# Attention and two MoE layers in one kernel: three engines ordered by hand in chunks 1 to 5, preparations in three steps, PV's quarters laid out anew

## The chip, the cores and the metric

The kernel runs on one core of a Trainium2 chip. The metric is the device time of one launch in microseconds; the kernel before took 836.0 us, the median of 3 runs (834.54 to 841.95).

In the text PE is TensorE, DVE VectorE, ACT ScalarE, POOL GpSimd, and SP SyncE, whose queue issues nearly all the transfers.

## What is computed

```python
def reference(q, k, v, x_params):                    # 4 batches, 8 heads, 576 positions, head size 64
    s = q @ k.T / 8 + alibi; s[outside 0 <= i - j < 128] = -1e9
    x = softmax(s) @ v                               # heads side by side: 2304 tokens x 512
    x = ((x @ w_a) * (x @ w_b)) @ w_out              # 512 -> 1536 -> 512
    logits = x @ w_gate + modality_bias[modality_id] # 8 experts
    e = argmax(logits); p = softmax(logits)[e]
    return p * (relu(x @ w1[e]) @ w2[e])             # 512 -> 1024 -> 512, each token its own expert
```

All of it is float32.

## The kernel before

The 2304 tokens are 18 tiles of 128, in seven chunks of 3, 2, 2, 3, 3, 3 and 2 tiles (0 to 6). In a chunk the first MoE layer runs in 12 **slots** j, one for each 128 of its 1536 hidden features. A slot multiplies the chunk's tokens with a piece of w_a into the PSUM bank ab0 (`mm_ab`, 12 matmuls of 256 or 384 columns, since every factor is split into a rounded part and a rest, and three of the four products are taken), then with w_b into ab1 (12 more). ACT copies ab0 (`asb`, L1050), DVE multiplies ab1 with it (`gf`, L1054), ACT and DVE split the product into two parts (`g`, L1057 and L1058), and one slot later `mm_out` (L512) multiplies these with a piece of w_out into the accumulators acc0 to acc2. There is one buffer each of ab0, ab1, asb and gf, so the next A (the matmuls into ab0) waits until asb has read ab0, and the next B until gf has read ab1. Chunk 0 works with unsplit products (L508), which chunk 0's own weights preparation slows.

The attention of chunk c + 1 runs inside the slots of chunk c. Its unit is an **item**: one pair of heads and one tile of 128 tokens, 72 in all. For an item PE computes scores (4 matmuls, L244), DVE masks them and takes the minimum (L252, L258), ACT takes the exponentials (L268), DVE the inverse sums (L272, L273), ACT divides (L281), PE transposes (2, L294), ACT and DVE split the result (`pc`, L305 and L306), POOL masks it into `pt` (two selects, L308 and L310), PE multiplies with v (PV, 4 matmuls, L374), ACT copies the result to `u` (L378, one copy of 128 x 512), two transfers take two quarters of u to the other 64 partitions (`z`), and POOL adds: two adds of 64 x 128 (L386), then z (L388). The sum `xf` has one buffer for a whole chunk; `x_split` (L397, L398) makes from it the two parts of the next chunk's tokens.

Each pair of heads first needs its **preparations**: ACT and DVE split k (`kk`, L190 and L191), q in two halves of 64 partitions (`qq`, L213 and L214) and v (`vv`, L225 and L226). `a_preps` makes all of them in a row.

When a chunk is done, `evac_out` copies its accumulators to `x2` (L593, three buffers). In chunks 0 to 5 DVE then takes the router's logits as dot products with rows of w_gate laid out over the partitions (`rd_dot`, L579: 8 for each tile; `wgt` comes two experts at a time, 512 KB, in the ring of buffers tagged "wo"). `route_fin` ranks each tile's tokens by expert with two small matmuls (L555, L556) and writes x2 to DRAM (`x2d`, L546). Only then is that x2 buffer free again.

The order on the engines comes from a scheduler of the framework, which goes by priorities and its own estimate of the times. SP issues transfers in the order of its queue, each after what it waits for. After chunk 6 the 8 experts follow, one after the other.

Of the kernel before, what the change touches and what calls it, by code (L numbers as in the profile page):

```python
# [21 lines left out]
def attn_moe_moe2(ctx: ExitStack, tc, q, k, v, moe_w_a, moe_w_b, moe_w_out, modality_id,  # L22
# [162 lines left out]
    def a_prep_k(a):  # L185
        if a.c in S32:
            return
# [3 lines left out]
        (nc.gpsimd if KLP else nc.vector).tensor_tensor(out=a.kk[:, :, 1, :n], in0=a.kr[:, :, :n], in1=a.kk[:, :, 0, :n], op=ALU.subtract)  # L191

    def a_prep_q(a):
        n = a.nt * P
        if a.c in S32:
            if a.c > 0:
                a.qq = at.tile([P, 2, MT * P], F32, tag="qq", bufs=2, name="qq")
            for h in range(2):
                o, d = 64 * h, 64 * (1 - h)
                if a.c > 0:  # L200
                    nc.gpsimd.memset(a.qq[d:d + 64, h, :n], 0.0)
                if a.c == 0 and a.hp < QD and h == 1:
                    nc.vector.tensor_scalar(out=a.qq[o:o + 64, h, :n], in0=a.qr[o:o + 64, :n],
                                            scalar1=qscale[o:o + 64, a.hp:a.hp + 1], scalar2=None, op0=ALU.mult)
                    continue
                nc.scalar.activation(out=a.qq[o:o + 64, h, :n], in_=a.qr[o:o + 64, :n], func=AF.Copy,
                                     scale=qscale[o:o + 64, a.hp:a.hp + 1])
# [8 lines left out]

    def a_prep_v(a):
        nk = a.nt + 1
# [3 lines left out]
        a.vv = at.tile([P, MT + 1, 2, 2, D], F32R, tag="vv", bufs=2, name="vv")  # L222

        w = a.vv.rearrange("p t h r d -> p t (h r) d")
        nc.scalar.copy(out=w[:, :nk, 0::3, :], in_=a.vr[:, :nk])  # L225
        nc.vector.tensor_tensor(out=w[:, :nk, 1:3, :], in0=a.vr[:, :nk], in1=w[:, :nk, 0::3, :], op=ALU.subtract)  # L226
# [1132 lines left out]
```

## Time and profile before

| | |
|---|---|
| median of 3 runs (range) | 836.0 us (834.54 to 841.95) |
| the profiled execution | 837.88 us |
| its span, first to last instruction | 836.1 us |
| mean granted clock of TensorE | 0.987 of full speed |
| PE busy | 805.8 us, 96% of the span |
| DVE, ACT, POOL busy | 564.9, 428.8, 273.6 us |
| A of slot 0 of chunks 1 to 6 starts at | 143.5, 208.6, 278.3, 373.2, 468.4, 548.6 us |

The rows are read so: a matmul's time runs from its issue to its modelled end, and the next one starts before that, so the pace of PE is the distance between starts, not the mean time of one. Of a wait the profile names the last thing that ended it.

### The profile page before, as it was taken

How to read it: one execution, taken by the hardware profiler on the slowest of the kernel's cores; microseconds unless marked ns; L12 is line 12 of the kernel's file. 1: busy time of each engine (PE TensorE's matmuls, PEld its weight loads, DVE VectorE, ACT ScalarE, POOL GpSimd, SP SyncE). 2: the span in 40 equal slices, each digit the busy share in tenths (PEclk: the TensorE clock that was granted, in tenths of full speed). 3: DMA queues.
4: the chain of work that ended last, by engine and by line, in shares of the span. 5: the costliest groups of instructions: out<-in, count | busy, mean ns of one | idle time of the engine just before them, and what ended most of it. 6: DMA issues, size and time to landing. Idle time of an engine off the chain costs nothing.

```text
span 836.1 us, 14442 instructions
## 1 busy us (share of the span) xinstructions
PE 805.8 (96%) x4666; PEld 723.4 (87%) x4666; DVE 564.9 (68%) x1699; ACT 428.8 (51%) x1092; POOL 273.6 (33%) x401
## 2 busy tenths in 40 slices
PE   8999999999989999999999999999999999999994
PEld 6788787898889989998999999999988998989893
...
GB/s 246 339 408 187 149 123 179 194 278 222 160 240 188 176 209 190 134 114 143 168 168 116 88 158 144 189 161 234 120 83 301 198 192 133 168 137 313 102 27 40
DMA packets 76196, 148.79 MB, mean 178 GB/s; under 512 B 13711, under 2 KB 40495, under 8 KB 76112
## 3 DMA queue, kind: packets, MB, share of 16 engines
...
q8 instruction: 39, 0.64, 0.3%
q14 instruction: 45, 0.37, 0.2%
HBM read 122.35 MB, written 22.12 MB: 173 GB/s over the span
## 4 chain that ended last, share of the span: by engine, by line
PE 72%; issue 8%; DMA 7%; ACT 4%; DVE 4%; POOL 2%; SPq 1%; POOLq 0%; ACTq 0%; DVEq 0%
PE ps_ab L495 32%; PE acc L512 13%; PE ps_h L1112 7%; PE ps_y L1095 6%; PE acc L508 3%; PE ps_o L374 3%; PE ps_s L244 2%; DMA wgt<-in_wgt 2%; DMA wr<-in_moe_w 1%; PE ps_p L294 1%; PE ps_o L331 1%; DMA wraw<-in_moe_w_b 1%; PE ps_s L240 1%; DMA wos<-wo_f 1%; POOL out L1102 1%
## 5 line engine op out<-in xcount | busy, mean ns | idle before, releaser
L495 PE MATMUL ps_ab<-xr,wab 128*128 128x384 f32 (+1 forms) x2016 | 347.3, 319 | 7.8 <-DVE gf L1054 3.6
L495 PEld LDWEIGHTS ps_ab<-xr,wab 128*128 128x128 f32 x2016 | 310.7, 189 | 21.3 <-DVE gf L1054 4.8
L512 PE MATMUL acc<-wo,g 128*128 128x512 f32 x540 | 145.7, 399 | 0.6 <-ACT g L1057 0.6
L512 PEld LDWEIGHTS acc<-wo,g 128*128 128x128 f32 x540 | 96.7, 189 | 16.2 <-ACT g L1057 0.8
L308 POOL TENSOR_SCALAR_AFFINE_SELECT pt<-pc 128x512 fp32r<-128x512 f32 (+1 forms) x72 | 51.4, 713 | 172.1 <-ACT pc L300 68.0
L1112 PE MATMUL ps_h<-xT,w1s 128*128 128x384 f32 x576 | 104.3, 337 | 0.0
L1095 PE MATMUL ps_y<-w2s,h 128*128 128x512 f32 x432 | 104.0, 394 | 0.0
L579 DVE CUSTOM_DVE_ANT_0 junk<-x,wgt 128x512 f32<-128x512 f32 x128 | 94.0, 735 | 12.4 <-DMA wgt<-in_wgt 10.1
L1112 PEld LDWEIGHTS ps_h<-xT,w1s 128*128 128x128 f32 x576 | 99.7, 188 | 1.4 <-issue 0.5
L1095 PEld LDWEIGHTS ps_y<-w2s,h 128*128 128x128 f32 x432 | 79.7, 188 | 15.8
L386 POOL TENSOR_TENSOR xf<-u 64x128 f32<-64x128 f32 x104 | 65.6, 631 | 38.3 <-ACT u L378 16.5
L268 ACT ACTIVATE p<-p,mx 128x128 f32<-128x128 f32 x144 | 56.9, 397 | 28.9 <-DVE mx L258 28.2
L1057 ACT CAST g<-gf 128x256 fp32r<-128x256 f32 (+1 forms) x72 | 33.0, 458 | 61.8 <-DVE gf L1054 61.7
...
L1054 DVE TENSOR_TENSOR gf<-ps_ab,asb 128x256 f32<-128x256 f32 (+1 forms) x72 | 35.0, 486 | 30.6 <-PE ps_ab L495 28.2
L868 DVE TENSOR_TENSOR w2s<-wr,w2s 128x1024 fp32r<-128x1024 f32 x24 | 29.4, 1224 | 38.1 <-ACT w2s L867 37.8
...
L1050 ACT COPY asb<-ps_ab 128x256 f32<-128x256 f32 (+1 forms) x72 | 30.5, 424 | 46.2 <-PE ps_ab L495 45.9
L310 POOL TENSOR_SCALAR_AFFINE_SELECT pt<-pc 128x512 fp32r<-128x512 f32 (+1 forms) x72 | 53.2, 739 | 0.0
L868 DVE TENSOR_TENSOR w1s<-wr,w1s 128x1024 fp32r<-128x1024 f32 x28 | 34.3, 1224 | 24.1 <-ACT w1s L867 24.1
L1058 DVE TENSOR_TENSOR g<-gf,g 128x256 fp32r<-128x256 f32 (+1 forms) x72 | 39.8, 553 | 10.0 <-ACT g L1057 9.7
L281 ACT ACTIVATE p<-p,mx 128x128 f32<-128x128 f32 x104 | 36.0, 397 | 20.5 <-DVE mx L273 20.1
...
## 6 DMA issues: line engine op xcount, KB each, us to landing
wo<-wo_d SPq DMA_DIRECT2D x60, 512.0 KB, 4.1
wr<-in_moe_w SPq DMA_DIRECT2D x56, 512.0 KB, 4.3
wgt<-in_wgt SPq DMA_DIRECT2D x24, 512.0 KB, 4.4
wraw<-in_moe_w_a SPq DMA_DIRECT2D x12, 512.0 KB, 7.6
wraw<-in_moe_w_b SPq DMA_DIRECT2D x12, 512.0 KB, 8.0
wor<-in_moe_w_out SPq DMA_DIRECT2D x12, 512.0 KB, 4.8
...
wo_d<-wo SPq DMA_DIRECT2D x12, 512.0 KB, 3.7
```

The lines of the kernel that those rows point to most:

```text
L268: nc.scalar.activation(out=it.p[:, h, :], in_=it.p[:, h, :], func=AF.Exp, bias=it.mx[:, 2 + h:3 + h], scale=-1.0, accum_out=it.mx[:, 4 + h ...
L281: nc.scalar.activation(out=it.p[:, h, :], in_=it.p[:, h, :], func=AF.Copy, scale=it.mx[:, 6 + h:7 + h])
L308: nc.gpsimd.affine_select(out=it.pt[:, :, 0], in_=pc, pattern=pat + [[-1, P]], base=0, channel_multiplier=1, compare_op=ALU.is_gt, fill=0.0)
L310: nc.gpsimd.affine_select(out=it.pt[:, :, 1], in_=pc, pattern=pat + [[1, P]], base=0, channel_multiplier=-1, compare_op=ALU.is_ge, fill=0.0)
L386: nc.gpsimd.tensor_tensor(out=xf_t[a.c][o:o + 64, a.hp, n], in0=u[o:o + 64, h, 0:P], in1=u[o:o + 64, h, P:2 * P], op=ALU.add)
L495: nc.tensor.matmul(ps[:, :n], lhsT=w[:, m, r, kk * P:(kk + 1) * P], rhs=xr[:, s, kk, :n], start=(idx == 0), stop=(idx == len(terms) - 1))
L512: nc.tensor.matmul(acc[c, t], lhsT=g[:, r, t * P:(t + 1) * P], rhs=w[:, s, :], start=(j == 0 and idx == 0), stop=(j == NJ - 1 and idx == 2))
L579: nc.vector.tensor_tensor_reduce(out=junk, in0=x2[:, 0:DM], in1=wgt[:, k], scale=1.0, scalar=0.0, op0=ALU.mult, op1=ALU.add, accum_out=lgr ...
L868: nc.vector.tensor_tensor(out=dst[:, 1], in0=srcw, in1=dst[:, 0], op=ALU.subtract)
L1058: nc.vector.tensor_tensor(out=gt[:, 1, :n], in0=gf[:, :n], in1=gt[:, 0, :n], op=ALU.subtract)
L1095: nc.tensor.matmul(pss[t], lhsT=h[:, r, f, t * P:(t + 1) * P], rhs=W2[f // 2][:, s_, f % 2, :], start=(f == 0 and i == 0), stop=(f == 7 an ...
L1112: nc.tensor.matmul(ps, lhsT=W1[f // 2][:, r, kk, (f % 2) * P:(f % 2 + 1) * P], rhs=xT[:, s_, kk, :], start=(kk == 0 and i == 0), stop=(kk ...
```

## The change

In chunks 1 to 5 the order on PE, DVE and ACT is no longer the scheduler's. `step` writes a slot down, and `tc.manual_schedule` keeps the three engines to the written order (chunks 0 and 6 and the experts stay with the scheduler, POOL and SP too). A slot is: A, PV of the items of two slots ago, B, transposes of the last slot's items, scores of new ones, mm_out, one piece of a router. The list `goal` says how many items each slot starts: 50 in chunks 1 to 5, about one a slot, and only in the first nine slots of chunk 5.

- **Preparations in three steps.** k's first half (ACT) in one slot, q's in the next, v's shortly before it is needed; the DVE half of each follows a slot later (`new_preps`, `late_rests`).
- **PV's quarters.** PV writes so that u needs three quarters of 64 partitions for each head: two ACT copies of 64 x 384 in place of one of 128 x 512. Both heads then lie in their own partitions, and POOL does one add of 128 x 128 in place of two of 64 x 128. The add of z goes behind the next item's selects (`z_add`).
- **Routers.** The 5 tiles of chunks 0 and 1 are routed on PE (`route(..., late=True)`: 4 transposes and 4 matmuls each) in place of 40 dot products. Chunks 2 to 5 keep the dots, an expert a slot in slots 1 to 8; wgt has buffers of its own, one expert (256 KB) each, fetched two ahead.
- **x2d later.** The write of x2 (`gate`) comes after the ranks, one tile a slot in slots 9 to 11, where it used to come at about slot 3 or 4.
- **Buffers.** xf is one tile for a pair of heads (5 buffers); w_out's splitting works in place.
- The loads of the first expert's w1 begin in chunk 6; before, the scheduler had put part of them into chunk 5.

```diff
-    RD = (0, 1, 2, 3, 4, 5)
+    RD = (2, 3, 4, 5)
...
     def a_pv(it):
...
-        u = at.tile([P, 2, 2 * P], F32, tag="u", bufs=2, name="u")
-        nc.scalar.copy(out=u, in_=ps)
+        u = at.tile([P, 3, P], F32, tag="u", bufs=2, name="u")
...
         for h in range(2):
-            o, d = 64 * h, 64 - 64 * h
-            nc.sync.dma_start(out=z[o:o + 64], in_=u[d:d + 64, h, 0:P])
-        for h in range(2):
             o = 64 * h
-            nc.gpsimd.tensor_tensor(out=xf_t[a.c][o:o + 64, a.hp, n], in0=u[o:o + 64, h, 0:P],
-                                    in1=u[o:o + 64, h, P:2 * P], op=ALU.add)
-        nc.gpsimd.tensor_tensor(out=xf_t[a.c][:, a.hp, n], in0=xf_t[a.c][:, a.hp, n], in1=z, op=ALU.add)
+            nc.scalar.copy(out=u[o:o + 64], in_=ps[o:o + 64, 1 - h:4 - h])
+        for h in range(2):
+            o, d = 64 * h, 64 - 64 * h
+            nc.sync.dma_start(out=z[o:o + 64], in_=u[d:d + 64, 1])
+        nc.gpsimd.tensor_tensor(out=xf_t[a.c, a.hp][:, n], in0=u[:, 0], in1=u[:, 2], op=ALU.add)
+        zq.append(lambda: nc.gpsimd.tensor_tensor(out=xf_t[a.c, a.hp][:, n], in0=xf_t[a.c, a.hp][:, n],
+                                                  in1=z, op=ALU.add))
...
+    def step(c, j, pend, sc, tp):
...
+        psa = mm_ab(c, j, 0)
+        for g in sc:
+            score_inv(live[g])
+        if c == 1:
+            wo_split(j)
+        for g in sc:
+            score_nrm(live[g])
+        late_rests()
...
+        nc.scalar.copy(out=asb[:, :n], in_=psa[:, :n])
+        if j == 0 and k:
+            evac(c - 1)
+        for g in tp:
+            a_pv(live.pop(g))
...
+        if now and DJ <= j < DJ + E:
+            rd_dot(j - DJ)
+            if j == DJ + E - 1:
+                rd_fin()
+        new_preps(goal[k + 2], goal[k])
...
+        psb = mm_ab(c, j, 1)
...
+        nc.vector.tensor_tensor(out=gf[:, :n], in0=psb[:, :n], in1=asb[:, :n], op=ALU.mult)
+        for g in sc:
+            pt_tr(live[g])
+        for g in new:
+            c_, hp_, t_ = items[g]
+            live[g] = score_mm(pairs[c_, hp_], t_)
...
+        for g in sc:
+            pt_cp(live[g])
+        z_add()
...
+        for g in new:
+            score_exp(live[g])
+        if pend is not None:
+            mm_out(*pend)
...
     for c in range(NC):
...
+                if c in (1, NC - 1):
+                    evac(c - 1)
```

**PE, the end of chunk 0.** Slot 11 of chunk 0 up to the start of chunk 1; ps_s are scores, ps_p transposes, ps_o PV (L374 and L412) and chunk 0's own attention; ps_ab is A or B, acc mm_out. Before:

```order
L495 MATMUL ps_ab_1643<-xr_131,wab_1536 128x384 x3
L294 MATMUL ps_p<-ident,p 128x128 x2
L495 MATMUL ps_ab_1643<-xr_131,wab_1536 128x384 x6
L294 MATMUL ps_p<-ident,p 128x128 x2
L374 MATMUL ps_o<-pt,vv 128x256 x4
L495 MATMUL ps_ab_1643<-xr_131,wab_1536 128x384 x3
L495 MATMUL ps_ab_1658<-xr_131,wab_1536 128x384 x12
L508 MATMUL acc_899<-f64f,gf 128x512
L374 MATMUL ps_o<-pt,vv 128x256 x4
L508 MATMUL acc_900<-f64f,gf 128x512
L508 MATMUL acc_901<-f64f,gf 128x512
L374 MATMUL ps_o<-pt,vv 128x256 x4
```

The change (L539 is the old L495, L552 the old L508, L412 the old L374):

```order
L539 MATMUL ps_ab_1646<-xr_131,wab_1538 128x384 x12
L539 MATMUL ps_ab_1661<-xr_131,wab_1538 128x384 x12
L552 MATMUL acc_899<-f64f,gf 128x512
L552 MATMUL acc_900<-f64f,gf 128x512
L552 MATMUL acc_901<-f64f,gf 128x512
L552 MATMUL acc_899<-f64f,gf 128x512
L552 MATMUL acc_900<-f64f,gf 128x512
L552 MATMUL acc_901<-f64f,gf 128x512
L539 MATMUL ps_ab_1703<-xr_1676,wab_515 128x256 x12
L412 MATMUL ps_o<-pt,vv 128x2x128 x4
L539 MATMUL ps_ab_1736<-xr_1676,wab_515 128x256 x12
```

Ahead of chunk 1 there stood 16 matmuls of scores (4 items), 6 transposes and 12 matmuls of PV for the coming chunks that now stand in chunk 1 or later; the last mm_out of chunk 0 stands ahead of chunk 1's first A.

**DVE, around a dot product.** Chunk 3, the logits of chunk 2's tiles (junk, lgr). Before:

```order
L1058 TENSOR_TENSOR g<-gf,g 128x384 [waits Activation_49]
L273 RECIPROCAL mx<-mx 128x2 [waits DVE_49] x2
L306 TENSOR_TENSOR pc<-ps_p,pc 128x2x128 [waits Activation_49]
L579 ISA junk,lgr<-x_3941,wgt 128x512 [waits DMAHW2_49,DVE_49]
L579 ISA lgr 128x1
L1054 TENSOR_TENSOR gf<-ps_ab_4216,asb 128x384 [waits DVE_49,PE_49]
L579 ISA junk,lgr<-x_3944,wgt 128x512 [waits DVE_49]
L579 ISA lgr 128x1
```

The change, also in chunk 3 (L637 is the old L579, L1144 the old L1054):

```order
L194 TENSOR_TENSOR kk<-kr_2_3499,kk 128x2x512 [waits DMAHW7_49,DMAHW6_49]
L637 ISA junk,lgr<-x_3886,wgt 128x512
L637 ISA lgr 128x1
L637 ISA junk,lgr<-x_3889,wgt 128x512 [waits DVE_49]
L637 ISA lgr 128x1
L1144 TENSOR_TENSOR gf<-ps_ab_4091,asb 128x384 [waits PE_49,Activation_49]
```

A dot that waits for a transfer (DMAHW) stood right ahead of gf; its wgt is now requested two slots earlier, and the two dots of a slot stand ahead of gf.

**ACT, chunk 6's first slots.** x_7227 and its like are the x2 copies of chunk 5's three tiles. Before:

```order
L867 CAST w1s<-wr_7340 128x1024 [waits DMAHW5_49]
L1057 CAST g<-gf 128x384 [waits DVE_49]
L1050 COPY asb<-ps_ab_7240 128x256 [waits PE_49,Activation_49]
L1057 CAST g<-gf 128x256 [waits DVE_49]
L593 COPY x_7227<-acc_6515 128x512 [waits PE_49]
L593 COPY x_7230<-acc_6516 128x512 [waits DMAHW4_49,PE_49]
L593 COPY x_7233<-acc_6517 128x512 [waits DMAHW6_49,PE_49]
L1050 COPY asb<-ps_ab_7345 128x256 [waits PE_49,Activation_49]
L1057 CAST g<-gf 128x256 [waits DVE_49]
```

The change (L652 is the old L593, L1240 the old L1050, L1245 the old L1057):

```order
L1156 CAST g<-gf 128x384 [waits DVE_49]
L443 CAST xr_7178<-xf_0_6177 128x256 [waits PE_49]
L443 CAST xr_7178<-xf_1_6388 128x256
L443 CAST xr_7178<-xf_2_6559 128x256
L443 CAST xr_7178<-xf_3_6855 128x256 [waits Pool_49]
L652 COPY x_7223<-acc_6451 128x512 [waits DMAHW3_49,PE_49]
L652 COPY x_7226<-acc_6452 128x512 [waits DMAHW5_49,PE_49]
L652 COPY x_7229<-acc_6453 128x512 [waits DMAHW7_49,DVE_49,PE_49]
L1240 COPY asb<-ps_ab_7234 128x256 [waits PE_49,Activation_49]
L1245 CAST g<-gf 128x256 [waits DVE_49]
L1240 COPY asb<-ps_ab_7341 128x256 [waits PE_49,Activation_49]
```

The three copies stand ahead of slot 0's asb and no longer behind it, and the third waits for a transfer and for DVE: its buffer is that of chunk 4's last tile, whose x2d write now comes at the end of chunk 5.

## Rows read from the trace of the kernel before

**Rows 1.** Stretches: length, busy time (x instructions) of PE, PEld, DVE, ACT, POOL; granted clock, DMA share, GB/s.

```profile
111.10:143.50 32.40, 32.40 (x168) 26.45 (x167) 28.35 (x73) 19.78 (x56) 6.94 (x10) 1.00 0.54 161
143.50:208.60 65.10, 62.06 (x428) 56.55 (x427) 55.63 (x184) 39.73 (x107) 27.76 (x37) 0.97 0.72 228
208.60:278.30 69.70, 65.62 (x478) 60.66 (x477) 54.08 (x191) 45.51 (x137) 37.79 (x58) 1.00 0.66 187
143.50:548.60 405.10, 393.96 (x2411) 364.11 (x2410) 294.32 (x996) 228.93 (x637) 181.44 (x268) 0.99 0.60 173
```

**Rows 2.** Timeline of PE, slots without attention, chunk 1: start, us, what ran.

```profile
177.09 2.98 PE L495 MATMUL ps_ab<-xr,wab 128*128 128x256 f32 x24
...
181.31 2.98 PE L495 MATMUL ps_ab<-xr,wab 128*128 128x256 f32 x24
```

**Rows 3.** The same in chunk 5.

```profile
490.16 4.33 PE L495 MATMUL ps_ab<-xr,wab 128*128 128x384 f32 x24
...
496.42 4.33 PE L495 MATMUL ps_ab<-xr,wab 128*128 128x384 f32 x24
```

**Rows 4.** The same for a slot with one item, chunk 1.

```profile
195.22 1.57 PE L495 MATMUL ps_ab<-xr,wab 128*128 128x256 f32 x12
196.63 0.64 PE L374 MATMUL ps_o<-pt,vv 128*128 128x256 f32 x4
197.11 0.63 PE L244 MATMUL ps_s<-kk,qq 128*128 128x256 f32 x4
197.58 0.99 PE L495 MATMUL ps_ab<-xr,wab 128*128 128x256 f32 x7
...
200.64 0.40 PE L495 MATMUL ps_ab<-xr,wab 128*128 128x256 f32 x2
```

**Rows 5.** Groups of PE by line, 143.5 to 548.6: count, busy time, mean of one.

```profile
L374 PE MATMUL ps_o<-pt,vv 128*128 128x256 f32 x196 | 34.9, 294 | 2.7 <-POOL pt L308 1.5 <-POOL pt L310 1.2
L244 PE MATMUL ps_s<-kk,qq 128*128 128x256 f32 x186 | 30.6, 288 | 0.0
L294 PE MATMUL ps_p<-ident,p 128*128 128x128 f32 x96 | 21.3, 274 | 0.1
```

**Rows 6.** What PE waited for, 143.5 to 548.6: us in total, times, longest.

```profile
PE ps_ab L495 <- DVE gf L1054: 3.6, 4, 1.6
PE ps_ab L495 <- ACT asb L1050: 2.9, 3, 1.8
```

**Rows 7.** Timeline of DVE in chunk 3; in brackets the idle time before and its releaser.

```profile
304.73 0.69 DVE L579 CUSTOM_DVE_ANT_0 junk<-x,wgt 128x512 f32<-128x512 f32 x1 [5.64 <-DMA wgt<-in_wgt]
...
305.35 0.55 DVE L1054 TENSOR_TENSOR gf<-ps_ab,asb 128x384 f32<-128x384 f32 x1
```

**Rows 8.** Timeline of PE where chunk 6's tokens are routed.

```profile
606.08 0.60 PE L524 MATMUL ps_x<-ident,x 128*128 128x128 f32 x4
606.44 1.29 PE L1112 MATMUL ps_h<-xT,w1s 128*128 128x384 f32 x6
...
609.05 0.95 PE L530 MATMUL ps_l<-wg,x2T 128*128 128x8 f32 x8
609.85 1.29 PE L1112 MATMUL ps_h<-xT,w1s 128*128 128x384 f32 x6
```

**Rows 9.** Groups of DVE by line, 143.5 to 548.6.

```profile
L579 DVE CUSTOM_DVE_ANT_0 junk<-x,wgt 128x512 f32<-128x512 f32 x104 | 77.5, 746 | 11.1 <-DMA wgt<-in_wgt 10.1 <-ACT x L593 0.2
```

**Rows 10.** Groups of ACT by line, 143.5 to 548.6.

```profile
L378 ACT COPY u<-ps_o 128x512 f32<-128x512 f32 x50 | 28.9, 584 | 21.6 <-PE ps_o L374 13.9 <-PE ps_r L556 1.8 <-PE ps_ab L495 1.8
...
L1050 ACT COPY asb<-ps_ab 128x384 f32<-128x384 f32 x36 | 17.1, 476 | 24.8 <-PE ps_ab L495 24.7
L213 ACT ACTIVATE qq<-qr,qscale 64x384 fp32r<-64x384 f32 x24 | 14.7, 613 | 0.3
```

**Rows 11.** Transfers by line: count, size, median us from issue to landing.

```profile
wgt<-in_wgt SPq DMA_DIRECT2D x24, 512.0 KB, 4.4
...
x2d<-x SPq DMA_DIRECT2D x18, 256.5 KB, 5.1
```

More of the change, by code (lines that the diff above doesn't have):

```diff
@@ new lines, in prep_qd, with prep_va @@
+    def prep_qd(a, h):
+        n, o, d = a.nt * P, 64 * h, 64 * (1 - h)
+        nc.vector.scalar_tensor_tensor(out=a.qq[d:d + 64, h, :n], in0=a.qr[o:o + 64, :n],
+                                       scalar=qscale[o:o + 64, a.hp:a.hp + 1], in1=a.qq[o:o + 64, h, :n],
+                                       op0=ALU.mult, op1=ALU.subtract)
+    def prep_va(a):
+        nk = a.nt + 1
+        a.vv = at.tile([P, MT + 1, 2, 2, D], F32R, tag="vv", bufs=2, name="vv")
+        a.vw = a.vv.rearrange("p t h r d -> p t (h r) d")
+        nc.scalar.copy(out=a.vw[:, :nk, 0::3, :], in_=a.vr[:, :nk])
@@ L193, in a_prep_q, with prep_vd, a_prep_k @@
+    def prep_vd(a):
+        nk = a.nt + 1
+        nc.vector.tensor_tensor(out=a.vw[:, :nk, 1:3, :], in0=a.vr[:, :nk], in1=a.vw[:, :nk, 0::3, :], op=ALU.subtract)
+    def a_prep_k(a):
+        if a.c not in S32:
+            prep_ka(a)
+            prep_kd(a)
     def a_prep_q(a):
         n = a.nt * P
-        if a.c in S32:
-            if a.c > 0:
-                a.qq = at.tile([P, 2, MT * P], F32, tag="qq", bufs=2, name="qq")
+        if a.c not in S32:
             for h in range(2):
[L199 to L207, printed above, removed]
+                prep_qa(a, h)
+                prep_qd(a, h)
@@ L221, in a_prep_v @@
             return
[L222 to L226, printed above, removed]
+        prep_va(a)
+        prep_vd(a)
     class Item:
@@ L362, in a_pv @@
         a, t = it.a, it.t
-        if a.c > 0 and a.c not in xf_t:
-            xf_t[a.c] = m1.tile([P, KD, MT * P], F32, tag="xf", bufs=1, name=f"xf{a.c}")
+        if a.c > 0 and (a.c, a.hp) not in xf_t:
+            xf_t[a.c, a.hp] = m1.tile([P, MT * P], F32, tag="xf", bufs=KD + 1, name=f"xf{a.c}_{a.hp}")
         if a.c in V32:
@@ L635, in a_loads, with late_rests, new_preps @@
             pos["load"] += 1
+    stage = {"k": [], "q": [], "d": []}
+    def late_rests():
+        for f in stage["d"]:
+            f()
+        stage["d"] = []
+    def new_preps(gk, gv):
+        d = stage["d"]
+        for a in stage["k"]:
+            for h in range(2):
+                prep_qa(a, h)
+                d.append(lambda a=a, h=h: prep_qd(a, h))
+        stage["q"] += stage["k"]
+        stage["k"] = []
+        while pos["prep"] < len(plist) and first[plist[pos["prep"]]] < gk:
+            a = pairs[plist[pos["prep"]]]
+            prep_ka(a)
+            d.append(lambda a=a: prep_kd(a))
+            stage["k"].append(a)
+            pos["prep"] += 1
+        while stage["q"] and first[stage["q"][0].c, stage["q"][0].hp] < gv:
+            a = stage["q"].pop(0)
+            prep_va(a)
+            d.append(lambda a=a: prep_vd(a))
     @hp
@@ L1009, in attn_moe_moe2, with evac @@
+    def evac(c):
+        for _ in evac_out(c):
+            pass
+        tr[:] = [[0, r] for r in tr]
+        now.extend(rd)
+        rd.clear()
+    pe = ExitStack()
     for c in range(NC):
```

273 lines of the change are left out of this document (178 added, 95 removed).

## The prediction

> **What bounds the kernel now.** I read the stretches first. From 143.5 to 548.6 us, the whole of chunks 1 to 5, PE is busy 393.96 of 405.10 us, while DVE has 294, ACT 229 and POOL 181 [rows 1]. So PE bounds, and nothing on another engine pays unless PE waits for it. Only two things can make this stretch shorter: fewer matmuls, or fewer places where the matmuls run apart.
>
> How much the second is worth needs a slot that nothing disturbs, for PE's busy time hides gaps inside a chain of matmuls. Where a slot holds no attention, A starts at 177.09 and the next A at 181.31: 4.22 us with 256 columns [rows 2]. With 384 columns it is 496.42 - 490.16 = 6.26 [rows 3]. A slot with one item runs from 195.22 to 200.64, 5.42, so an item costs 1.20: PV 197.11 - 196.63 = 0.48, scores 0.47, and the other 0.25 I give to the transposes [rows 4].
>
> From these I build the stretch as it would be if nothing waited. 24 slots x 4.22 + 36 x 6.26 = 326.7. The items: 186 matmuls of scores are about 47 items, 96 transposes 48, 196 matmuls of PV 49 [rows 5]; 47 x 0.47 + 48 x 0.25 + 49 x 0.48 = 57.6. 13 tiles are ranked with two small matmuls each, at 0.10 apiece (eight small matmuls take 609.85 - 609.05 = 0.80 [rows 8]): 2.6. Sum 386.9. The stretch took 405.1, so **18.2 us** of it are waits and stretches at a lower clock. The table of waits accounts for a part by name: 3.6 us for gf, 2.9 for asb [rows 6], 2.7 for the selects [rows 5]. The clock was 0.97 in chunk 1 and 1.00 in chunk 2 [rows 1].
>
> What such a wait is made of can be seen at 304.73: DVE had sat idle 5.64 us before a dot product whose wgt had not landed, and the gf behind it, for which PE waited, came at 305.35 [rows 7]. The gf was ready to run; it stood in the wrong place of the queue. That is the kind of loss a written order can remove.
>
> **The change part by part, on PE.**
>
> 1. The 18.2 us. A wait of this kind vanishes if the instruction stands later than what it needs. The change puts each on a distance of a slot or more: wgt is asked for two experts ahead (a slot is at least 4.2 us and a landing of 512 KB took 4.4 [rows 11], half of that size now), preparations are spread over slots, PV stands two slots behind its scores. I count all 18.2 as gone: **-18.2**, and price new waits apart.
> 2. Items. 50 scores, 51 transposes and 52 PVs stand in the stretch now, 3 of each more: 3 x 1.20 = **+3.7** with rounding.
> 3. Those matmuls come out of chunk 0's end, and one more item's scores with them: 16 scores, 6 transposes, 12 PVs. At 0.12 for a matmul of scores or PV (0.48 / 4) and 0.12 for a transpose that is 28 x 0.12 + 6 x 0.12 = 4.1. From 111.1 to 143.5 PE was busy all 32.40 us [rows 1], so taking matmuls away shortens it: **-4.0**.
> 4. Routers on PE. Four transposes kept PE from 606.08 to 606.44, eight passes of the small matmuls from 609.05 to 609.85 [rows 8]: 0.36 + 0.80, about 1.2 a tile, five tiles **+6.0**. Bounds: 5.0 if the weight loads hide better, 7.8 by the busy times 0.60 + 0.95.
> 5. DVE loses 40 dots of 0.746 [rows 9], 29.8 us. DVE is not the bound, so I count nothing. If its queue is what delays gf, the gain is in item 1 already.
>
> So far -18.2 + 3.7 - 4.0 + 6.0 = **-12.5**.
>
> **What is given back.** Where the change makes PE wait anew:
>
> - Chunk 6, slot 1. The third x2 copy needs its buffer free, and the write that frees it now comes at the end of chunk 5: rank, then about 0.8 us on DVE (its gate stands behind four splits), then 5.1 to land [rows 11], so 5.9 after the chunk's start, the copy 0.5, and asb, queued behind it, 0.3. A of slot 1 may start at 6.8 and is due 4.95 after the start (a clean 4.22 plus the 0.7 of chunk 5's longer mm_out): **+1.9**.
> - Chunk 5, slot 1. The same copy stands behind asb there, with the u copies, preparations and pc behind it. asb is on time; pc is late by about 2 us, selects follow, and PV of slot 1 waits: **+1.0** (0 to 2).
> - Chunks 3 and 4, first slots: slot 0 has no mm_out, so the selects have less time: **+0.5** together.
> - Chunks 1 and 2, where slots are 5.4 us and ACT is fullest: **+1.0** (0 to 5, see the second rival).
> - Chunk 6: two dots at a time, wgt in the queue behind the loads of the experts: **+0.8**.
>
> Sum **+5.2**, bounds 2 and 10.
>
> u needs two ACT copies of 384 columns for one of 512. The old one took 0.584, a PSUM copy of 128 x 384 0.476, the nearest row with 64 partitions, qq, 0.613 [rows 10]. Two cost 0.95 to 1.23, so +0.37 to +0.64 for each of 52 items, 19 to 33 us of ACT. I take 0.476 each, for asb too is a plain copy out of PSUM, while qq reads a scale and writes the rounded type. It is hidden: ACT was busy 229 of 405 us [rows 1]. The Trainium skill speaks against this edit, "Perfetto Trace Analysis", section on optimizing Scalar/DVE operations: every ScalarE instruction pays a fixed access overhead, about 51 ns on PSUM, and grouping into larger operations helps if the engine is saturated. The rows agree in kind: 128 columns more cost only 0.108 [rows 10], and three times that is 0.32, so 0.15 of the 0.476 is fixed. ACT is at 61% in chunk 1 and 65% in chunk 2, not saturated.
>
> POOL has one add less for each item; it is not waited for except at its selects, so I count nothing, and the z add now stands behind the next selects, where no PV waits for it.
>
> **Sum.** -12.5 + 5.2 = -7.3. The profiled execution took 837.9, 1.9 above the median, so 830.6 of it, and 828.7 on the median's scale. I round to **828.5**.
>
> **The rivals.**
>
> *Nothing is given back (0.25).* If the x2d writes land faster or ACT has more slack than I reckon, -12.5 to -11 remain: 825.4 to 826.9 of the profiled execution, 823.5 to 825 of the median. For it: most slots of chunks 3 to 5 already ran undisturbed in the old order. Against: the buffer wait at chunk 6 is plain in the order.
>
> *ACT sets the pace in chunks 1 and 2 (0.13).* If a copy of u costs 0.61 as qq does, an ACT slot of the 21 with an item gains 0.64, and ACT there was busy 39.7 + 45.5 = 85 of 135 us [rows 1] with its work waiting in a ring (exponentials, DVE, divide, transposes, pc). The ring then is 0.2 to 0.3 us longer than the slot of 5.42: 21 x 0.25 = 5 us on top, 833.7, up to 836.
>
> *Slower: PV waits for the selects in every slot (0.12).* PV stands right behind A, ahead of B, so when pt is late the whole slot is. Before, the scheduler could put PV where its data were; PE waited for selects only twice, 2.7 us [rows 5]. In a fixed order a chain to the selects that is too long costs its lateness in each of 50 items. The place is PV behind A, the price 50 x the lateness: from 7.3 / 50 = 0.15 us on the gain is gone, from (7.3 + 8.4) / 50 = 0.31 the kernel is over 1% slower, and at 0.4 it stands at 828.7 + 20 = 849. Against it: a whole A and an mm_out, over 2.8 us, lie between B's end and PV.
>
> *The change does not do what it says (0.08).* If the waits come from transfers that are late on SP's queue, whatever the order, most of the 18.2 stays: 834 to 838. For it: the wait of rows 7 is one for a transfer, 10.1 us of DVE's idle time stand before dots for wgt [rows 9]. Against: they were requested late, in the ring of w_out's pieces.
>
> **Chances.** The likeliest case, as summed, has 0.42, from 826 to 832. A measurement of this kernel can tell about 1% from no change, so faster means below 827.6 and slower above 844.4. The likeliest case lies below 827.6 with 0.19, the first rival wholly: faster 0.44. The rest of the likeliest, the second and fourth rivals: same 0.44. Slower 0.12. The range takes in the first rival with the bounds of the routers and of the matmuls moved (some 2 us more), the second and the fourth, and leaves out the slower one: 821 to 838; the likeliest alone 826 to 832.
>
> **What would show it.** In the trace after, the starts of A should lie 5.4 us apart in chunks 1 and 2 and 7.5 in 3 and 4 with one item each; from chunk 1's first A to chunk 6's some 400 us; chunk 0's last four slots 28 to 29 us and chunk 0's mm_out behind them. PE's waits should name asb or the x2 copy near chunk 6's slot 1 (some 2 us), and no gf behind a dot. The u copies should take 0.48; at 0.6 the second rival is live. If PV shows waits for L310's successor in many slots, the slower rival holds. I would be wrong in the sum if the 18.2 were not waits but a clean pace that the old slots could reach only without attention.

## The result, and the profile after

The changed kernel took 842.4 us, the median of 20 runs (840.2 to 844.4), the kernel before, in 20 runs beside it, 835.2. The ratio is 1.0076, 95% interval 1.0059 to 1.0092: a little slower. The prediction was 828.5 with a range of 821 to 838, so the time lies outside the range and on the other side.

| profiled execution | before | after |
|---|---|---|
| time | 837.88 us | 843.18 us |
| span | 836.1 | 840.9 |
| PE busy | 805.8 | 813.1 |
| DVE, ACT, POOL busy | 564.9, 428.8, 273.6 | 546.7, 461.2, 236.1 |
| first A of chunk 1 / 2 / 3 | 143.5 / 208.6 / 278.3 | 141.4 / 212.0 / 284.1 |
| first A of chunk 4 / 5 / 6 | 373.2 / 468.4 / 548.6 | 375.0 / 466.0 / 549.9 |

The stretches of the kernel after, with the columns of [rows 1]: the end of chunk 0, chunks 1, 2, 3 and 5, and all of chunks 1 to 5.

```profile
110.90:141.40 30.50, 30.50 (x139) 23.43 (x138) 20.67 (x43) 11.12 (x29) 1.49 (x2) 1.00 0.40 119
141.40:212.00 70.60, 68.33 (x500) 63.03 (x499) 47.68 (x163) 53.26 (x147) 29.04 (x42) 1.00 0.62 196
212.00:284.00 72.00, 70.72 (x503) 64.13 (x502) 47.05 (x162) 53.69 (x151) 28.31 (x47) 1.00 0.58 164
284.00:375.00 91.00, 90.80 (x522) 84.25 (x522) 62.74 (x208) 62.06 (x163) 34.02 (x53) 1.00 0.64 171
...
466.00:549.90 83.90, 82.98 (x461) 76.92 (x460) 54.65 (x175) 36.26 (x96) 20.27 (x29) 1.00 0.45 123
141.40:549.90 408.50, 403.55 (x2504) 372.62 (x2503) 281.42 (x929) 267.14 (x719) 145.27 (x219) 1.00 0.56 158
```

Against [rows 1], chunk 0's end is 1.9 us shorter although it now holds the last mm_out of chunk 0 (2.6 us by the old trace, six passes of 0.43), so 4.5 less. Chunk 1 is 5.5 longer and chunk 2 2.3, while chunks 3 and 4 are each some 4 us shorter, with PE busy for 90.8 of 91.0. The written order works there: slots 2 to 8 start 7.48 us apart, one like the other (A at 312.75, 320.23 and 327.71). But work has moved too: PE runs 72 matmuls more in chunk 1 and 25 more in chunk 2 than before, routers and items, and some 16 fewer in each of chunks 3 and 4. Taken chunk by chunk, the recipe of the prediction (a clean slot, the items, the routers) puts the time above the clean pace in chunks 1 to 5 at about 6, 5, 4, 3 and 1 us before and 4, 5, 1, 1 and 2 after, an estimate. So chunks 1 and 2 are longer because they hold more work, and most of their waits did not go. The granted clock was 1.00 in all of chunks 1 to 5, so it is no part of this.

What PE waited for in the whole kernel after (columns of [rows 6]; L412 is PV, L345 the second select, L539 A and B, L556 mm_out):

```profile
PE ps_o L412 <- POOL pt L345: 2.7, 8, 0.7
PE ps_ab L539 <- DVE gf L1243: 1.6, 1, 1.6
PE ps_ab L539 <- ACT asb L1240: 1.6, 1, 1.6
...
PE acc L556 <- ACT g L1156: 1.5, 2, 0.9
```

The waits for gf and asb are now in chunk 6. In chunks 1 to 5 it is PV that waits for the selects and, in the last slots of chunks 1 and 2, mm_out that waits for g.

### The profile page after: what moved, and what is told of

Same layout as the page of the kernel before. It is cut to its first block, busy times and chain, and to the rows that moved or that the text cites. A ratio compares the mean times of both kernels' runs of the same rounds, so it can differ in the third digit from the quotient of the medians.

```text
span 840.9 us, 14490 instructions
## 1 busy us (share of the span) xinstructions
PE 813.1 (97%) x4726; PEld 728.0 (87%) x4726; DVE 546.7 (65%) x1619; ACT 461.2 (55%) x1149; POOL 236.1 (28%) x349
## 4 chain that ended last, share of the span: by engine, by line
PE 65%; DMA 9%; ACT 8%; issue 8%; DVE 5%; POOL 2%; SPq 1%; POOLq 0%; ACTq 0%; DVEq 0%
PE ps_ab L539 26%; PE acc L556 10%; PE ps_h L1291 9%; PE ps_y L1274 8%; PE acc L552 4%; PE ps_o L412 2%; PE ps_s L268 2%; DMA wraw<-in_moe_w_b 2%; ACT u L419 2%; DMA kk<-in_k 1%; ACT p L292 1%; DMA x2d<-x 1%; ACT qq L200 1%; PE ps_p L327 1%; DMA qr<-in_q 1%
## 5 line engine op out<-in xcount | busy, mean ns | idle before, releaser
L539 PE MATMUL ps_ab<-xr,wab 128*128 128x384 f32 (+1 forms) x2016 | 339.2, 318 | 3.3 <-DVE gf L1243 1.6
L539 PEld LDWEIGHTS ps_ab<-xr,wab 128*128 128x128 f32 x2016 | 309.1, 189 | 12.1 <-issue 2.2
L556 PE MATMUL acc<-wo,g 128*128 128x512 f32 x540 | 138.7, 398 | 1.5 <-ACT g L1156 1.5
L556 PEld LDWEIGHTS acc<-wo,g 128*128 128x128 f32 x540 | 96.6, 188 | 20.6 <-ACT g L1156 2.3
L343 POOL TENSOR_SCALAR_AFFINE_SELECT pt<-pc 128x512 fp32r<-128x512 f32 (+1 forms) x72 | 53.8, 747 | 176.0 <-DVE pc L341 109.8
L1144 DVE TENSOR_TENSOR gf<-ps_ab,asb 128x384 f32<-128x384 f32 (+1 forms) x60 | 30.3, 504 | 64.4 <-PE ps_p L327 43.4
L637 DVE CUSTOM_DVE_ANT_0 junk<-x,wgt 128x512 f32<-128x512 f32 x88 | 62.6, 711 | 8.9 <-DMA wgt<-in_wgt 4.2
L423 POOL TENSOR_TENSOR xf<-u 128x128 f32<-128x128 f32 x52 | 25.6, 492 | 128.5 <-ACT u L419 128.5
L419 ACT COPY u<-ps_o 64x384 f32<-64x384 f32 x104 | 49.5, 476 | 3.2 <-PE ps_o L412 2.0
L345 POOL TENSOR_SCALAR_AFFINE_SELECT pt<-pc 128x512 fp32r<-128x512 f32 (+1 forms) x72 | 49.9, 693 | 0.0
L1294 ACT ACTIVATE h<-ps_h 128x384 fp32r<-128x384 f32 x48 | 23.6, 492 | 45.4 <-PE ps_h L1291 43.0
L1123 ACT COPY asb<-ps_ab 128x384 f32<-128x384 f32 (+1 forms) x60 | 25.9, 431 | 33.9 <-PE ps_ab L539 33.7
L1295 DVE SCALAR_TENSOR_TENSOR h<-ps_h,h 128x384 fp32r<-128x384 f32 x48 | 26.4, 555 | 27.9 <-ACT h L1294 27.9
```

The costliest lines, as they stand in the source:

```text
L343: nc.gpsimd.affine_select(out=it.pt[:, :, 0], in_=pc, pattern=pat + [[-1, P]], base=0, channel_multiplier=1, compare_op=ALU.is_gt, fill=0.0)
L345: mark["pt"] = nc.gpsimd.affine_select(out=it.pt[:, :, 1], in_=pc, pattern=pat + [[1, P]], base=0, channel_multiplier=-1, compare_op=ALU.i ...
L419: nc.scalar.copy(out=u[o:o + 64], in_=ps[o:o + 64, 1 - h:4 - h])
L539: nc.tensor.matmul(ps[:, :n], lhsT=w[:, m, r, kk * P:(kk + 1) * P], rhs=xr[:, s, kk, :n], start=(idx == 0), stop=(idx == len(terms) - 1))
L556: nc.tensor.matmul(acc[c, t], lhsT=g[:, r, t * P:(t + 1) * P], rhs=w[:, s, :], start=(j == 0 and idx == 0), stop=(j == NJ - 1 and idx == 2))
L637: nc.vector.tensor_tensor_reduce(out=junk, in0=x2[:, 0:DM], in1=w, scale=1.0, scalar=0.0, op0=ALU.mult, op1=ALU.add, accum_out=lgr[:, e:e ...
```

## The experiments

### Preparations behind pc

One slot of chunk 2 shows what makes the selects late. The timeline of the kernel after (start, us, engine, what ran, in brackets the idle time before): L200 are two halves of q's preparation, L340 and L341 pc, L343 and L345 the selects, L412 PV.

```profile
245.51 1.23 ACT L200 ACTIVATE qq<-qr,qscale 64x384 fp32r<-64x384 f32 x2
...
246.76 0.37 ACT L340 CAST pc<-ps_p 128x256 fp32r<-128x256 f32 x1
...
247.17 0.42 DVE L341 TENSOR_TENSOR pc<-ps_p,pc 128x256 fp32r<-128x256 f32 x1 [1.09 <-ACT pc L340]
...
247.67 0.86 POOL L343 TENSOR_SCALAR_AFFINE_SELECT pt<-pc 128x512 fp32r<-128x512 f32 x1 [1.93 <-DVE pc L341]
...
248.48 0.63 POOL L345 TENSOR_SCALAR_AFFINE_SELECT pt<-pc 128x512 fp32r<-128x512 f32 x1
...
248.58 0.39 PE L412 MATMUL ps_o<-pt,vv 128*128 128x256 f32 x1
...
249.17 0.62 PE L412 MATMUL ps_o<-pt,vv 128*128 128x256 f32 x3 [0.20 <-POOL pt L345]
```

The transposes that pc needs were done at about 245.1. ACT was in qq until 246.7, so pc began at 246.76, and the second select ended at 249.1. PV's place came at about 248.4, for A had started at 246.88 and a PV that waits for nothing starts 1.5 us behind it (A at 228.51, PV at 230.03); its last operand came some 0.7 us late. The slot took 6.38 us, and 5.50 in the run below. `step` writes the preparation ahead of pc, and ACT takes them in that order. In a slot of 256 columns there is no slack for it.

```diff
-        new_preps(goal[k + 2], goal[k])
...
         nc.vector.tensor_tensor(out=gt[:, 1, :n], in0=gf[:, :n], in1=gt[:, 0, :n], op=ALU.subtract)
+        new_preps(goal[k + 2], goal[k])
```

> One line moved: on ACT the preparations (kk, qq, vv first halves) stand behind the copies pc and g of a slot, no longer ahead of them, so the ACT order in a slot is asb, u, u, pc, g, preparation, exponentials. In the trace of the changed kernel, slot 6 of chunk 2 shows pc waiting behind two qq activations of 0.61 us (pc at 246.76, transposes done at 245.2), then the selects end at 249.1 and PV, due at 248.27, comes 0.9 late. Theory A (the preparation ahead of pc makes the selects late): in chunks 1 and 2, where the slots hold some 11 us more than clean ones, 6 to 8 us go, chunk 1 plus chunk 2 fall from 142.6 to about 135, and the time falls by about 7 us, to about 835. Theory B (ACT is simply too full in chunks 1 and 2, its ring of work is longer than a slot): the order matters little, the same lateness comes back through the exponentials, and the time stays within 2 us of 842. Theory C (POOL's selects themselves, or the transfers on the way, are late): no change either, and PV still waits for the second select.

The line moves behind g as well as behind pc. Measured: 838.6 us, ratio to before 1.0040 (1.0015 to 1.0065). Chunks 1, 2 and 5 of this kernel:

```profile
141.60:209.10 67.50, 67.29 (x501) 62.87 (x499) 45.40 (x162) 51.97 (x146) 27.20 (x43) 1.00 0.64 201
209.10:276.90 67.80, 67.62 (x504) 63.48 (x502) 44.63 (x163) 53.00 (x152) 28.40 (x46) 1.00 0.66 179
458.40:545.60 87.20, 84.49 (x460) 78.40 (x460) 54.77 (x175) 35.73 (x96) 20.12 (x29) 0.98 0.41 119
```

Chunks 1 and 2 fell from 142.6 to 135.3, as theory A said, with the same work on the same engines. So ACT is not too full (theory B), and POOL is not the cause (theory C). PE is busy 134.9 there against 139.05 with the same matmuls: of the 7.3 us that went, 4.1 had stood as busy time and not as a wait. By the starts of A, eight slots became 0.3 to 1.1 us shorter, and the last slots of the two chunks 1.2 and 1.0. In these last slots it was not PV that had waited but mm_out, for g, which stood behind the same qq (kernel after, end of chunk 1):

```profile
208.42 1.24 ACT L200 ACTIVATE qq<-qr,qscale 64x384 fp32r<-64x384 f32 x2
...
210.08 0.41 ACT L1156 CAST g<-gf 128x256 fp32r<-128x256 f32 x1
...
210.54 1.66 PE L556 MATMUL acc<-wo,g 128*128 128x512 f32 x6 [0.94 <-ACT g L1156]
```

The ratio as a whole fell only from 1.0076 to 1.0040, some 3 us, for chunk 5 grew from 83.9 to 87.2. Its timeline on ACT (L652 the x2 copies, L419 u, L340 pc):

```profile
461.16 1.07 ACT L652 COPY x<-acc 128x512 f32<-128x512 f32 x2
...
465.18 0.59 ACT L652 COPY x<-acc 128x512 f32<-128x512 f32 x1 [2.95 <-DMA x2d<-x]
465.66 0.97 ACT L419 COPY u<-ps_o 64x384 f32<-64x384 f32 x2
...
466.66 0.37 ACT L340 CAST pc<-ps_p 128x256 fp32r<-128x256 f32 x1
```

The third x2 copy waits 2.95 us for an x2d write that was issued at 459.12, and u and pc queue behind it. PV then waits 2.50 us. For a while after that wait the granted clock (third column from the end) is at its lower level, 0.50 of full speed or 1.2 GHz, so the slot grew by more than the wait, from 8.94 to 12.18:

```profile
466.00:468.50 2.50, 0.08 (x1) 0.00 (x0) 1.39 (x6) 2.41 (x7) 1.38 (x3) 1.00 0.14 30
...
470.00:471.50 1.50, 1.50 (x6) 1.50 (x6) 1.44 (x4) 1.48 (x5) 0.00 (x0) 0.50 0.01 5
```

### The x2d write a slot earlier, alone and with the first edit

```diff
-        if ranks and ranks[0][0] == 1:
+        while ranks and ranks[0][0] == 1:
             next(ranks.pop(0)[1], None)
```

> All tiles whose logits are ready are ranked at the end of a slot, no longer one a slot, so the last x2d write of chunks 2 to 5 comes a slot earlier (slot 10). Theory (the x2 buffer that waits for its x2d write holds up ACT): the wait of PE for asb in chunk 6 (1.6 us, the slot 1.7 over clean) and the 1.5 us in chunk 5's slot 1 go, 2 to 3 us in all, about 839.5. Rival (these waits come from something else at the turn of the chunks, such as the missing mm_out in slot 0 or the u copies behind it): chunk 6's goes and chunk 5's stays, 1.5 us, or neither.

Measured alone: 843.1 us, ratio 1.0095 (1.0060 to 1.0130), no gain. Chunk 6's slot 0 became 1.7 us shorter, but its slots 3 and 6 became 1.2 and 0.9 longer in its place, and chunk 5's slot 1 was still 1.1 over a clean one. There qq stood ahead of pc again and no x2 copy waited; the rival had the outcome right.

> The edits of e1 (preparations behind pc and g on ACT) and of e5 (all ready tiles ranked at a slot's end) together. In e1 chunks 1 and 2 lost 7.3 us, but chunk 5 grew from 83.9 to 87.2: in its slot 0 ACT sat idle 2.95 us at the third x2 copy, released by an x2d write, with the u copies and pc behind it. In e5 alone the x2 copies moved little in the total. Theory: two separate mechanisms, the preparation ahead of pc and the x2 buffer; together chunk 5 falls to about 82.5, chunk 6's slot 0 loses its 1.5, and the time is 838.6 - 5 to 6, about 833. Rival: chunk 5's 4.9 us in slot 1 come from the new place of the preparation and not from x2d: chunk 5 stays at 87, and the time at about 838.

Measured together: 833.9 us, ratio 0.9981 (0.9964 to 0.9999). Chunk 5:

```profile
457.50:540.80 83.30, 82.88 (x461) 77.00 (x460) 54.32 (x176) 35.80 (x97) 19.96 (x29) 1.00 0.44 125
```

83.3, from 87.2: two mechanisms, and in chunk 5 neither edit shows its worth without the other (83.9 with neither, 87.2 with the first, 84.0 with the second).

### One copy of u, as before

```diff
-            nc.scalar.copy(out=u[o:o + 64], in_=ps[o:o + 64, 1 - h:4 - h])
+        nc.scalar.copy(out=u, in_=ps)
...
-        nc.gpsimd.tensor_tensor(out=xf_t[a.c, a.hp][:, n], in0=u[:, 0], in1=u[:, 2], op=ALU.add)
+            nc.gpsimd.tensor_tensor(out=xf_t[a.c, a.hp][o:o + 64, n], in0=u[o:o + 64, 1 - h],
+                                    in1=u[o:o + 64, 3 - h], op=ALU.add)
```

> Undoes the part of the change on u: one ACT copy of 128x512 out of PSUM (0.584 us in the trace of before) in place of two of 64x384 (0.476 each in the trace of the change), and on POOL two adds of 64x128 again in place of one of 128x128. Saves 0.37 us of ACT for each of 52 items, just ahead of the preparation and pc. Theory A (preparation ahead of pc): pc comes 0.37 earlier in each slot, PV's lateness of 0.3 to 0.9 us in about 14 slots shrinks by as much, 3 to 5 us. Theory B (ACT too full): the 21 items of chunks 1 and 2 give 0.37 each, about 8 us. Theory C (POOL late): POOL has 0.4 us more for each item ahead of the next selects, so no gain or a loss of 1 to 3 us.

Measured: 842.7 us, ratio 1.0109 (1.0070 to 1.0149). No gain: chunk 1 grew to 74.0, chunk 2 fell to 70.9. By the starts of A two things happened, and they nearly cancel. Slots 4 and 7 of both chunks grew, by 8.6 us together; in each of them POOL sat idle for 1.7 to 3.6 us before its second add, in three of the four by name for a scatter into `tab` (explained below). POOL's adds in chunks 1 and 2 of this kernel:

```profile
L423 POOL TENSOR_TENSOR xf<-u 64x128 f32<-64x128 f32 x42 | 19.9, 475 | 57.7 <-ACT u L417 45.3 <-DMA tab<-tokid,po_all 8.4 <-DVE mx L298 2.6
```

Of the other slots, those that the preparation had made late became shorter by 6.4 us together and as short as in e1, though the preparation still stands ahead of pc. So the 0.37 us that the second copy of u adds to ACT was not hidden: taking it out did nearly what moving the preparation does. That is read from the starts in one trace of each kernel; no run has the single copy without the second add.

Each of the two copies takes what I had taken from the plain PSUM copy (group of ACT by line, kernel after):

```profile
L419 ACT COPY u<-ps_o 64x384 f32<-64x384 f32 x104 | 49.5, 476 | 3.2 <-PE ps_o L412 2.0
```

The same edit on top of the mended order, and of one dot a slot in chunk 6 (below):

> e10 with one u copy of 128x512 and POOL's two adds, as in e2. In the trace of the change each u copy of 64 partitions took 0.476, so the two cost 0.37 more than the one of 0.584, 19 us of ACT in all. Theory (ACT has room once the preparations stand behind pc): no difference, within 1.5 us of e10. Rival 1 (ACT still sets the pace in some slots): 2 to 4 us faster than e10. Rival 2 (POOL's second add makes the selects late, as chunk 1 of e2 may show, 74.0 against 70.6): 1 to 3 us slower.

Measured: 846.4 us, ratio 1.0100 (1.0060 to 1.0141), 1.2% over the same kernel without it; chunk 1 went from 67.5 to 75.6. The second rival had the direction and the size was far off. The timeline of POOL and PE in slot 4 of chunk 1 (L423 the adds, L343 and L345 the selects, L412 PV):

```profile
161.26 0.48 POOL L423 TENSOR_TENSOR xf<-u 64x128 f32<-64x128 f32 x1
...
164.59 0.54 POOL L423 TENSOR_TENSOR xf<-u 64x128 f32<-64x128 f32 x1 [2.86 <-DMA tab<-tokid,po_all]
...
165.21 0.64 POOL L343 TENSOR_SCALAR_AFFINE_SELECT pt<-pc 128x512 fp32r<-128x512 f32 x1
165.80 0.63 POOL L345 TENSOR_SCALAR_AFFINE_SELECT pt<-pc 128x512 fp32r<-128x512 f32 x1
...
165.90 0.39 PE L412 MATMUL ps_o<-pt,vv 128*128 128x256 f32 x1 [1.44 <-POOL pt L343]
```

Between the first add and the second POOL sits idle for 2.86 us until a scatter into `tab`, issued at 159.53, has landed. The built program says why; these are three of its rows on POOL:

```
L619 DMA tab<-tokid,po_all 21632x16 [waits DVE_49]
L423 TENSOR_TENSOR xf_2_2086<-u 64x128 [waits Activation_49]
L423 TENSOR_TENSOR xf_2_2086<-u 64x128 [waits DMASW1_49,Pool_49]
```

The second add carries a wait for the scatter's semaphore. In the program of the change no add on POOL carries one. Why the framework sets it on the second add was not tried. So the single add is worth far more than the 0.5 us of POOL that it saves. In chunk 1 all of the loss lies in the two slots with such a wait, 3.7 and 4.4 us, and part of it is the clock: PE had nothing for 1.4 us in the first and 2.4 in the second, and then worked for some 3 us at the lower level (0.50, 1.2 GHz). The stretches of slot 4 with the wait and after it, columns of [rows 1]:

```profile
164.40:165.90 1.50, 0.06 (x1) 0.00 (x0) 0.42 (x1) 0.37 (x1) 1.23 (x3) 1.00 0.94 369
...
169.00:170.50 1.50, 1.50 (x8) 1.50 (x8) 0.50 (x2) 0.41 (x2) 0.12 (x1) 0.50 0.20 41
```

### The new quarters in the kernel before

> The kernel before with the part on PV's quarters alone: PV writes the new layout, two ACT copies of 64x384, one POOL add of 128x128, then z; the order left to the scheduler. I priced this part at nothing. In e14, where the old layout came back under the order by hand, the second add of 64x128 waited 2.9 and 3.8 us for the landing of a scatter (tab), selects and PV behind it, and chunks 1 and 2 lost 11 us. In the trace of before the same wait stands once, 2.38 us at 202.38, and PE waits 1.2 us for the select behind it. Theory (the second add carries a wait for the scatter, and the scheduler moves PV out of its way): the part by itself is worth 0 to 2 us, 833 to 835. Rival (ACT's 19 us more weigh, or a new order of the scheduler): 1 to 5 us slower.

The edit is the part of the diff from `ps = ps_at.tile` to the add, put into the kernel before. Measured: 831.3 us, ratio 0.9962 (0.9941 to 0.9983): faster. Chunks 2 and 4:

```profile
205.70:271.30 65.60, 64.78 (x475) 60.27 (x474) 51.06 (x185) 49.62 (x147) 29.94 (x46) 1.00 0.68 199
...
366.20:458.10 91.90, 90.63 (x530) 84.35 (x527) 68.86 (x239) 60.07 (x166) 36.53 (x53) 1.00 0.49 143
```

They took 69.7 and 95.2 before. The adds on POOL, before and in this kernel, with what ended their idle time:

```profile
L386 POOL TENSOR_TENSOR xf<-u 64x128 f32<-64x128 f32 x103 | 64.8, 629 | 38.3 <-ACT u L378 16.5 <-DVE xr L398 11.9 <-DMA tab<-tokid,po_all 5.9
```

```profile
L385 POOL TENSOR_TENSOR xf<-u 128x128 f32<-128x128 f32 x51 | 28.9, 571 | 27.2 <-ACT u L381 17.5 <-DVE xr L396 7.7 <-DVE mx L272 2.0
```

The 5.9 us behind tab are gone from the list; they were four waits in the trace of before, not the one that I had expected. That this accounts for all of the gain is argued, not shown: in the profiled executions chunks 1 to 5 are 6 us shorter, the medians lie 3.5 apart, and the scheduler's order is another one throughout.

### The routers

> The router of chunks 0 and 1 goes back to dot products on DVE (40 more, one expert a slot), so PE loses the five tiles' transposes and matmuls, which I priced at 1.2 us each, 6.0 in all. If that price is right and DVE has room for the dots (47 of 70 us busy in chunk 1), chunks 1 and 2 get 5 to 6 us shorter, time about 837. If the dots, three a slot in chunk 1 (2.2 us) right ahead of gf, make gf or pc late, the gain is eaten: within 2 us of 842, with PE waiting for gf.

Edit: `RD = (0, 1, 2, 3, 4, 5)`. Measured: 849.5 us, ratio 1.0177 (1.0148 to 1.0206). By the price of the prediction PE was rid of some 6 us, and the kernel was 7 slower. Chunk 1, and what PE waited for in chunks 1 and 2:

```profile
139.60:217.10 77.50, 70.00 (x464) 61.74 (x463) 63.05 (x204) 51.89 (x144) 28.16 (x41) 0.98 0.66 204
```

```profile
PE ps_o L412 <- POOL pt L345: 4.0, 18, 0.4
PE ps_o L412 <- POOL pt L343: 3.6, 7, 1.3
```

DVE is busy 63 of 77.5 us, and 25 waits for the selects take 7.6.

> e8 with the router of chunks 0 and 1 back on DVE, as in e3: PE has 6.0 us less, DVE 40 dots more, ahead of gf. In e3 PV waited for the selects 29 times, 9.4 us. Theory X (those waits were the preparation ahead of pc, made worse): they go here, and the time is about 6 us below e8, 826. Theory Y (the dots themselves hold up DVE, so that the DVE half of pc and the maxima come late): PV goes on waiting, chunks 1 and 2 stay above e8's by 2 to 6 us, 834 to 838.

Measured, on top of the mended order: 846.4 us, ratio 1.0141 (1.0097 to 1.0185), 13 us above the same kernel without the dots. Theory X falls: the dots hold up DVE by themselves, and more than Y allowed for; PE then also waits for the ranks.

> The kernel before with one number changed: the router of chunks 0 and 1 on PE, the order left to the scheduler. It prices that part of the change by itself. PE gets 5 x 1.2 = 6.0 us more, DVE 29.8 less. If the old order's 18 us of waits came in good part from dots in the wrong place of DVE's queue, chunks 1 and 2 lose some of their 8 and 7.5 us and the sum is about zero, 834 to 837. If the dots had little to do with those waits, it is 840 to 842, and the PE router alone accounts for most of what the change lost.

Edit: `RD = (2, 3, 4, 5)` in the kernel before. Measured: 836.9 us, ratio 1.0016 (0.9995 to 1.0037). If PE's price of 6.0 holds here too, 4 to 5 us of it were paid back by DVE's relief. That relief was to be had in the old order, without a written one.

### Chunk 6

> e7, and in chunk 6 the start of the experts (their first loads on SP's queue) stands behind the slot's dot products and so behind the requests for wgt 4 and 5. In the trace of the change DVE sat idle 3.77 us at a dot for wgt, with gf behind it, and PE waited 1.6 for gf. Theory: wgt was late because it was requested behind the experts' loads; the dot no longer waits, 1 to 2 us go, about 831.5. Rival: the loads of w1 come that much later, the casts of w1 on ACT, with asb behind them, wait longer, or the first expert waits for its w1: no gain, or up to 4 us slower than e7.

Edit: the block from `if j == EJ` moved behind the dots. Measured: 833.2 us, ratio 0.9979 (0.9959 to 1.0000), no different from 0.9981. PE's wait for gf in chunk 6 did not go but grew, from 1.3 to 2.6, and chunk 6 up to slot 11 took 53.0 in place of 51.5:

```profile
PE ps_ab L539 <- DVE gf L1232: 2.6, 1, 2.6
```

> e7, and in chunk 6 one expert's dot products a slot in slots 0 to 7 in place of two in slots 0 to 3, so that each wgt is asked for two slots (8.4 us) ahead. In e7 chunk 6 still takes 51.5 us against 49.2 before: PE waits 1.3 us for a gf behind a dot whose wgt is late, and 1.4 for asb behind casts of w1 whose loads are late. Theory: the wait for gf goes, the waits for asb stay, chunk 6 falls by 1 to 1.5, time 832.5. Rival: the ranks come four slots later, and the first expert, which needs them, or chunk 6's own router starts later: the gain is given back behind chunk 6, time 834 or more.

Edit: `rd_dot(j)` for j below 8 in place of two dots for j below 4. Measured: 836.9 us, ratio 0.9984 (0.9960 to 1.0009). No wait for gf is left in chunk 6, but PE now waits in slot 2 for tokens gathered for the first expert (ps_t, transposes that the scheduler put there):

```profile
PE ps_t L1004 <- DMA xg<-x2d,idx: 1.8, 1, 1.8
PE ps_t L1004 <- issue: 1.1, 1, 1.1
```

Slot 2 took 10.9 us in place of 4.2, with the granted clock at 0.72 in the mean, and chunk 6 up to slot 11 took 54.1. The gain was given back, in chunk 6 and not behind it as the rival had it.

```diff
-        wgt[e] = m1.tile([P, DM], F32, tag="wgt", bufs=2, name="wgt")
+        wgt[e] = m1.tile([P, DM], F32, tag="wgt", bufs=3, name="wgt")
...
-        if e + 2 < E:
-            rd_fetch(e + 2)
+        if e + 3 < E:
+            rd_fetch(e + 3)
```

> e7 with three buffers for wgt and the rows of w_gate requested three experts ahead. In e7 chunk 6 takes 51.5 us, 2.3 more than before; PE waits there 1.3 us for a gf behind a dot whose wgt is late. Theory (wgt is asked for too late for two dots a slot): this wait goes, chunk 6 falls to about 50, the time to 0.996 or 0.997 of before. Rival (in chunk 6 everything that comes over SP's queue is late together, w1's pieces first, so gf and asb wait behind the casts of w1 anyway): chunk 6 stays at 51 to 52 and the ratio at that of e7, 0.998.

Measured: 831.4 us, ratio 0.9953 (0.9935 to 0.9971), the lowest of all, though its interval overlaps those of e7 (0.9981) and e16 (0.9962), so that the step itself shows only in the trace. Chunks 1 to 5, then chunk 6 up to slot 11, and PE's waits in both:

```profile
141.30:542.10 400.80, 399.23 (x2505) 372.36 (x2504) 275.91 (x936) 262.25 (x719) 141.37 (x220) 1.00 0.57 162
542.10:591.90 49.80, 48.77 (x347) 44.39 (x346) 35.95 (x128) 16.52 (x39) 6.27 (x6) 1.00 0.63 206
```

```profile
PE ps_ab L539 <- ACT asb L1240: 0.8, 1, 0.8
...
PE ps_ab L539 <- DVE gf L1243: 0.3, 1, 0.3
```

Chunk 6 is down from 51.5 to 49.8, as the theory said.

## Why the prediction was wrong

- **The 18.2 us of waits: right that they can go.** The same recipe for the kernel after gives 326.7 + 61.2 for 52 PVs, 50 scores and 51 transposes + 6.0 + 2.6 - 0.7 for the piece of mm_out at the end = 395.8. With the preparations and x2d mended chunks 1 to 5 take 400.8, which is 5.0 above the recipe, where the kernel before stood 18.2 above its own. So the clean pace is real but for these 5.0, which no run takes apart.
- **The step that failed: what is given back in chunks 1 and 2, priced at 1.0 with bounds 0 and 5.** The kernel after took 408.5 for its 395.8, so 12.7 us of waits are there, where I had 2.5 for chunks 1 to 5. By the estimate above some 9 of them are in chunks 1 and 2, which had held some 11 before. 7.3 of the 12.7, in chunks 1 and 2, came from one line, preparations ahead of pc and g; four later kernels with that line moved (e7, e8, e10 and e15) have chunks 1 and 2 at 67.5 and 67.8 again. I had compared ACT's busy sum with the slot and called the copies of u hidden. What counted was the order: the row of ACT in a slot is asb, u, u, preparation, pc, g, and in the slot shown pc's data are there 1.7 us before ACT comes to it. The two copies of u stand in that row too, and with one copy in their place (e2) most of those slots were on time. It was to be seen in the order of the change, and I had listed what stands behind a waiting instruction only at the turns of the chunks.
- **The slower rival had the place.** PV waited for the selects, but by what e1 made shorter in eight slots of chunks 1 and 2 and not in all 50; in two more mm_out waited for g, which no rival named. I had set against it that an A and an mm_out lie between B's end and PV; with 256 columns that is 2.8 us, and a preparation, pc and two selects are longer, 3.6 in the slot shown (245.51 to 249.11).
- **Items, chunk 0's end: right.** Chunk 0's end became 4.5 us shorter, against 4.0.
- **The routers: right on PE, DVE's dots not priced by themselves.** In chunk 1 the transposes of a tile take 0.36 us of PE (145.83 to 146.19) and the eight passes 0.81 (152.24 to 153.05), 1.17 against 1.2. DVE's 40 dots I counted at nothing, with their worth inside the 18.2. In the old order they were worth 4 to 5 us, if PE's price holds; in the written order, which cannot move around them, 7 us net and more, though PE is spared 6.
- **u: the price of ACT was right (0.476 each), but it was not hidden, and the worth of the single add was missed.** It was put at nothing; in the old order the part is worth 3.5 us, in the mended one 9.5, the lower clock behind the waits included.
- **Chunk 6: the asb wait 1.6 against 1.9, the gf wait 1.6 against 0.8.** Both in their places. But in e5 the first went and others took its place, for the wait is only the nearest of several.
- **Chunk 5's slot 1: size near (1.5 against 1.0), cause wrong.** In the kernel after no x2 copy waited there; the write had landed within 3.6 us, and ACT went without a gap from the three x2 copies (468.64) over u and qq to pc (472.40). The same write took 6.1 us in e1, and then it did.

On the profiled execution -7.3 was forecast and +5.3 measured, 12.6 apart: 12.7 - 2.5 = 10.2 us lie in chunks 1 to 5. Of the other 2.4, the part behind the start of slot 11 of chunk 6 grew by 1.1 (238.3 to 239.4) and the time outside the span by 0.5; 0.8 is left to the turns of the chunks and the spread of these readings.
